# Keys turned with the heads innermost, moved in one piece, and read by the scores with a stride of 16 numbers

## The chip, the cores and the metric

The kernel runs on one core of a Trainium2 chip. The metric is the time of one execution on the device in microseconds (us), as the median of several runs; lower is better. One execution was recorded by the hardware profiler, and the views below come from it.

## The reference

There are two blocks, one after the other. The first is a gated linear attention over 4 batches, 8 heads, 768 steps and 48 numbers a head: a complex gate of magnitude at most 0.999 multiplies a 48 x 48 state at each step, and the query reads the state. The second is a layer of 3072 tokens, 384 numbers and 2048 hidden units, gated by the cosine.

```python
mag = np.sqrt(a_re * a_re + a_im * a_im)
scale = np.minimum(mag, 0.999) / (mag + 1e-06)
a_re_n, a_im_n = (a_re * scale, a_im * scale)
for t in range(S):
    ar, ai = (a_re_n[:, :, t, :, None], a_im_n[:, :, t, :, None])
    new_re = ar * S_re - ai * S_im
    new_im = ar * S_im + ai * S_re
    kv = np.einsum('bhd,bhe->bhde', k[:, :, t], v[:, :, t])
    S_re, S_im = (new_re + kv, new_im)
    y[:, :, t] = np.einsum('bhd,bhde->bhe', q[:, :, t], S_re)
...
h = x @ w_in            # x: y with the heads side by side
g = h * np.cos(h)
return (g @ w_out)
```

## The kernel before

The steps are cut into 24 chunks of 128, and two chunks make a group, so there are 12 groups (`G` = 2, `NG` = 12). Within a chunk the recurrence becomes matrix products. The gates are summed up as logarithms and angles, the keys are divided and the queries multiplied by the products of the gates, and each is stacked with its cosine and sine part into 96 numbers a head: `ks` and `qs`, 128 steps by 16 heads (8 heads of two chunks) by 96. The scores of a head (`sc`, `f_scores`) are the product of its turned keys and turned queries over the 96 numbers; VectorE masks them (`atm`), and they multiply `v` (`yp`, `f_out`). What came before the chunk is carried in `state` (`sp`, `state_sums` and `state_next`). The result goes through DRAM into `xT`, and then through the layer: `hp` (`mm1_sums`), the gate (sine and square on ScalarE, `gate_product` on VectorE), and the second product as `op` and `sum`, which from group 2 on is formed from seven products of half size.

`hp` of a group is made in eight pairs of 12 matmul records each; from group 2 on the three PSUM buffers of the pool `pm` are taken in turn, so the fourth pair needs the buffer of the first. Each fp32 matmul appears as two records, and so does each weight load.

The scores need the keys and queries turned, with the 96 numbers over the partitions and the 128 steps in a row. For groups 0 and 1 (`g < PEG`) TensorE turns them (`f_turn`), and ScalarE copies them out of PSUM. For groups 2 to 11 `f_transpose` does it in three steps, keys first, then queries:

- VectorE turns blocks of 32 x 32 into `tr`: 128 partitions (four quarters `q` of 32 steps, `r` within the quarter being one of the 96 numbers by threes), `NB` = 3 blocks, 16 heads `x`, 32 steps `j`.
- A DMA from the SP queue writes `tr` to DRAM, as `moved`, ordered by quarter and by number.
- DMAs from the SP queue read it back into `kT` or `qT`, 96 partitions.

`kT` is stored as heads, quarters, steps, so that the 128 columns of a head lie side by side; this takes four DMAs, one for each quarter. `qT` is stored as quarters, heads, steps and takes one; a head's 128 steps are then four runs of 32. In the scores `kT` is the stationary operand, and `qT` the moving one:

```python
matmul(ps[:, h], lhsT=X[n // G]["kT"][:, n % G * H + head],
       rhs=queries(n, head), start=True, stop=True)
```

`kT`, `qT` and `tr` have one, one and two buffers, `moved` three. TensorE's order is written out by `chain` in `matmul`. From group 2 on the program is woven: `weave` gives each part of a group's round a place between 0 and 1 and sorts by it. The scores of group n (`chunks(n)`) lie at the start, the layer's `hp` (`first(n)`) at 0.56 to 1, and the turning for group n + 1 (`keys(n + 1)`) at about 0.53 to 0.64, beside the first pairs of `hp`. VectorE and ScalarE take what the scheduler gives them in that order. SP's queue holds all loads, the transfers of the turning, those of `xT` and the stores.

Of the kernel before, what the change touches and what calls it, by code (L numbers as in the profile page):

```python
# [11 lines left out]
F32 = mybir.dt.float32  # L12
# [475 lines left out]
def fast_path(ctx, tc, q, k, v, a_re, a_im, moe_w_in, moe_w_out, out, least, odd, wide,  # L488
# [7 lines left out]
    nc = tc.nc  # L496
    B, H, S, D = q.shape
    DM, DF = moe_w_in.shape
    C = 128
    NCH = S // C  # L500
    G = 2
    N = B * NCH
    NG = N // G
    D2 = 2 * D
    HH = H // 2
    ND = DM // C
    Q4 = C // 32
    NB = D2 // 32
# [7 lines left out]
    ft = ctx.enter_context(tc.tile_pool(name="ft", bufs=2))  # L516
    msb = ctx.enter_context(tc.tile_pool(name="msb", bufs=2))
    rows_d = ctx.enter_context(tc.tile_pool(name="rows_d", bufs=2, space=bass.MemoryType.DRAM))
# [18 lines left out]
    def chain(ins, engine="scalar"):  # L537

        if engine in tail:
            behind(ins, tail[engine])  # L540
        tail[engine] = ins

    def behind(ins, other):
        tc.add_manual_dep(ins.ins, other.ins.name, mybir.DependencyInfo(
            mybir.DependencyClass.NoSync, mybir.DependencyReason.DATA))
# [14 lines left out]
    X = [dict() for _ in range(NG)]  # L560
# [4 lines left out]
    PEG, PER = 2, 1  # L565
# [118 lines left out]
    vector, scalar = Ordered(nc.vector, "vector"), Ordered(nc.scalar, "scalar")  # L684

    def matmul(out, **kw):
        chain(nc.tensor.matmul(out, **kw), "tensor")  # L687
# [233 lines left out]
    def f_transpose(g, i, n, name):  # L921


        if i == 0:
            X[g][name] = ft.tile([D2, G * H, Q4, 32] if name == "kT" else [D2, Q4, G * H, 32], F32,
                                 tag=name, name=name, bufs=1)
        tr = ft.tile([C, NB, n * H, 32], F32, tag="tr", name="tr")
        turn = vector.transpose(out=tr, in_=X[g][name[0] + "s"][:, ds(i * H, n * H)].rearrange(
            "p x a d -> p x (a d)").rearrange("p x (r b) -> p b x r", b=NB))
        if name == "qT" and "gated" in X[g - 1]:  # L930
            behind(turn, X[g - 1]["gated"])
        moved = rows_d.tile([Q4, D2, n * H, 32], F32, tag="moved", name="moved", bufs=3)
        nc.sync.dma_start(out=moved.rearrange("q (r b) x j -> (q r) b x j", b=NB), in_=tr)
        if name == "kT":
            for q4 in range(Q4):
                nc.sync.dma_start(out=X[g][name][:, ds(i * H, n * H), q4], in_=moved[q4])
        else:
            nc.sync.dma_start(out=X[g][name][:, :, ds(i * H, n * H)],
                              in_=moved.rearrange("q c x j -> c q x j"))

    def f_turn(g, i, name, hh):

# [9 lines left out]
    def queries(n, h):  # L952
        g, i = divmod(n, G)
        if g < PEG:
            return X[g]["qT"][:, i * H + h].rearrange("p q j -> p (q j)")
        return X[g]["qT"][:, :, i * H + h]

    def f_scores(n, hh):
        y = Y[n]
        if hh == 0:  # L960
            y["atm"] = ft.tile([C, H, C], F32, tag="atm", name="atm")
        ps = pa.tile([C, HH, C], F32, tag="a", name="sc")
        for h in range(HH):
            head = hh * HH + h
            matmul(ps[:, h], lhsT=X[n // G]["kT"][:, n % G * H + head],
                   rhs=queries(n, head), start=True, stop=True)
        y["masked"] = vector.tensor_tensor(
            out=y["atm"][:, ts(hh, HH)], in0=ps, in1=causal.unsqueeze(1).to_broadcast([C, HH, C]), op=ALU.mult)

    def f_out(n):  # L970
        y, (g, i) = Y[n], divmod(n, G)
        vals = X[g]["v"][:, i]
        state = y.get("state")
        if i == 0:
            X[g]["yT"] = ft.tile([C, HH, G, C], F32, tag="yT", name="yT", bufs=1)
        ps = pa.tile([C, HH, C], F32, tag="a", name="yp")
        for p in range(HH):
            for side in range(2):
                matmul(ps[ds(side * 64, D), p], lhsT=vals[:, 2 * p + side],
                       rhs=y["atm"][:, 2 * p + side], start=True, stop=(state is None))  # L980
            if state is not None:
                for side in range(2):
                    matmul(ps[ds(side * 64, D), p], lhsT=state[:, 2 * p + side],
                           rhs=queries(n, 2 * p + side), start=False, stop=True)
        for side in range(2):
            half = ds(side * 64, D)
            scalar.copy(out=X[g]["yT"][half, :, i], in_=ps[half])

    def f_rows(n, lo=0, hi=H):

        y, (g, i) = Y[n], divmod(n, G)
        state = y.get("state")
        if lo == 0:
            y["yr"] = pa.tile([C, H, D], F32, tag="a", name="yr")
        ps = y["yr"]
        for h in range(lo, hi):
            matmul(ps[:, h], lhsT=y["atm"][:, h], rhs=X[g]["v"][:, i, h],
                   start=True, stop=(state is None))
            if state is not None:
                matmul(ps[:, h], lhsT=queries(n, h), rhs=state[:, h], start=False, stop=True)  # L1000
        if hi < H:
            return
        y["rows"] = msb.tile([C, DM], F32, tag="ot", name="rows")
        scalar.copy(out=y["rows"], in_=ps.rearrange("p h d -> p (h d)"))
# [221 lines left out]
    def keys(g):  # L1226

        if not 0 <= g < NG:
            return
        for i, n in spans(g):  # L1230
            yield lambda i=i, n=n: g_trig(g, i, n)
            yield lambda i=i, n=n: (g_stack(g, i, n), p_end(g, i, n))
            for name in "kT", "qT":
                if g >= PEG:
                    yield lambda i=i, n=n, name=name: f_transpose(g, i, n, name)
# [24 lines left out]
    def chunks(g):  # L1260
        for n in range(g * G, g * G + G):
            for hh in range(2):
                yield lambda n=n, hh=hh: f_scores(n, hh)
            yield lambda n=n: f_state(n)
            yield lambda n=n: f_out(n)
        yield lambda: (f_x(g), f_xt(g))
        if g + 2 < NG:
            yield lambda: load(g + 2, ("k", "q", "v"))
# [101 lines left out]
    lows(0, 1)  # L1370
    piece(0)
    f_scores(0, 0)
    f_scores(0, 1)
    turn(0, 1)
    piece(0, 1, 0, 1)
# [302 lines left out]
```

## Time and profile before

| what | us |
|---|---|
| median of 3 runs | 655.88 |
| lowest and highest | 655.13, 659.32 |
| the profiled execution | 653.01 |
| its span in the trace | 651.2 |
| TensorE busy | 641.0 |
| VectorE busy | 492.0 |
| ScalarE busy | 392.8 |
| one turning of keys on VectorE, x10 | 2.252 |
| one issue of a kT DMA on SP, median, x40 | 1.323 |
| one issue of a qT DMA on SP, median, x10 | 1.185 |

Busy time is the sum of an engine's records; records of TensorE overlap, and the ends of its matmuls are modelled, so its pace is better read from the starts of successive records. In the profile, PE is TensorE's matmul, PEld its weight load, DVE is VectorE, ACT ScalarE, and SPq the DMA issue on SyncE's queue. Most operations go through two helpers and so carry line L687 (matmuls) or L676 (VectorE and ScalarE); tile names tell them apart. A group of records shows its count, then busy time and the mean length of one in ns, then the idle time ahead of it and what ended that idle time.

### The profile page before, as it was taken

To read this page: it belongs to the slowest core of one execution; us is meant where nothing else is said; L and a number is where in the kernel's file an instruction comes from. 1 tells how busy PE (TensorE), PEld (TensorE's weight loads), DVE (VectorE), ACT (ScalarE), POOL (GpSimd) and SP (SyncE) were. 2 spreads that over 40 slices of the span, in tenths; PEclk is the share of its full clock that TensorE was granted. 3 is DMA by queue.
4 is the path that set the end of the run, shared out by engine and by line. 5 is a ranking of instruction groups with operands and counts; after the bars stand their busy time and mean duration, and the time that the engine had idled before them with its cause. 6 is when DMAs were issued, how large, how long until landed. Compare 5 with 4: busy or idle time off the path is not lost.

```text
span 651.2 us, 10758 instructions
## 1 busy us (share of the span) xinstructions
PE 641.0 (98%) x4075; PEld 576.4 (89%) x4075; DVE 492.0 (76%) x799; ACT 392.8 (60%) x726; POOL 30.9 (5%) x53
## 2 busy tenths in 40 slices
PE   8999999999999999999999999999999999999997
PEld 6888877777999999899899899899899999999996
DVE  6999989888687688786787787876877878862251
ACT  7898687284583593494494485485576476433330
POOL 4010200000000000010010010000000000000000
PEclk9999999999999999999999999999999999999999
DMA  9968755727627656747738737836836843363001
GB/s 249 244 179 203 225 164 123 170 62 182 146 49 182 158 146 148 194 110 167 209 82 191 204 85 167 205 96 151 226 105 146 219 123 98 112 134 120 25 1 31
DMA packets 232920, 94.90 MB, mean 146 GB/s; under 512 B 208701, under 2 KB 221246, under 8 KB 232858
## 3 DMA queue, kind: packets, MB, share of 16 engines
q1 hardware_dynamic: 225320, 68.51, 45.3%
q0 software_dynamic: 5824, 25.50, 11.7%
q8 instruction: 34, 0.56, 0.4%
q10 hardware_dynamic: 1714, 0.11, 0.2%
q14 instruction: 28, 0.23, 0.1%
HBM read 69.28 MB, written 24.81 MB: 144 GB/s over the span
## 4 chain that ended last, share of the span: by engine, by line
PE 92%; ACT 4%; DVE 3%; DMA 0%; issue 0%; SPq 0%; DVEq 0%
PE hp L687 38%; PE op L687 18%; PE sum L687 16%; PE sc L687 6%; PE yp L687 6%; PE sp L687 4%; PE phs L687 2%; PE lgs L687 1%; ACT tan L707 1%; PE yr L687 1%; PE tp L948 1%; ACT rs L707 1%; ACT lg L707 1%; ACT L703 1%; DVE mag L676 1%; DVE atm L676 1%
## 5 line engine op out<-in xcount | busy, mean ns | idle before, releaser
L687 PE MATMUL hp<-xT,w_in 128*128 128x256 f32 (+1 forms) x1176 | 252.5, 375 | 0.0
L687 PEld LDWEIGHTS hp<-xT,w_in 128*128 128x128 f32 x1176 | 219.6, 190 | 30.2 <-issue 0.2
L707 ACT ACTIVATE gate<-hp,half_pi_b 128x512 f32<-128x512 f32 x96 | 66.0, 687 | 118.5 <-PE hp L687 118.5
L687 PE MATMUL op<-w_out,gate 128*128 128x192 f32 (+1 forms) x448 | 100.7, 374 | 0.0
L676 DVE TENSOR_TENSOR gate<-hp,gate 128x512 f32<-128x512 f32 x96 | 65.7, 684 | 45.8 <-ACT junk L676 45.7
L687 PEld LDWEIGHTS op<-w_out,gate 128*128 128x128 f32 x448 | 75.9, 190 | 16.9 <-issue 2.0
L676 ACT ACTIVATE junk<-hp 128x512 bf16<-128x512 f32 x96 | 56.7, 591 | 0.0
L687 PE MATMUL sum<-t_s,s 128*128 128x192 f32 x320 | 56.3, 329 | 0.0
L687 PEld LDWEIGHTS sum<-t_s,s 128*128 128x128 f32 x320 | 52.1, 190 | 1.5 <-issue 1.5
L676 DVE TENSOR_TENSOR atm<-sc,causal 128x512 f32<-128x512 f32 x48 | 32.9, 689 | 23.4 <-PE sc L687 23.4
L687 PEld LDWEIGHTS sc<-qT,kT 96*128 96x128 f32 x384 | 47.4, 192 | 2.3 <-issue 0.6
L687 PE MATMUL sc<-qT,kT 96*128 96x128 f32 x384 | 49.0, 276 | 0.2 <-ACT qT L676 0.2
L676 ACT ACTIVATE ot<-sum 128x192 f32<-128x192 f32 x39 | 12.6, 322 | 53.7 <-PE sum L687 53.4
L676 DVE SCALAR_TENSOR_TENSOR ot<-op,ot 128x192 f32<-128x192 f32 x40 | 13.3, 354 | 38.0 <-PE op L687 36.4
L687 PE MATMUL yp<-atm,v 128*48 128x128 f32 x352 | 33.6, 277 | 0.9 <-ACT Q L707 0.6
L703 ACT ACT_TABLE_LOAD x24 | 30.8, 1283 | 1.2 <-PEq L1662 0.7
L676 ACT COPY yT<-yp 48x512 f32<-48x512 f32 x44 | 25.3, 574 | 7.4 <-PE yp L687 7.0
L687 PE MATMUL yp<-qT,state 96*48 96x128 f32 x304 | 29.7, 272 | 0.0
L687 PE MATMUL sum<-w_out,gate 128*128 128x192 f32 x160 | 29.7, 329 | 0.0
L687 PE MATMUL sp<-v,ks 128*96 128x48 f32 x320 | 29.7, 245 | 0.0
L687 PEld LDWEIGHTS sp<-v,ks 128*96 128x96 f32 x320 | 29.6, 165 | 0.0
L676 ACT CAST tan<-phs 128x384 int32<-128x384 f32 x24 | 11.4, 480 | 29.4 <-PE phs L687 29.4
(147 smaller groups left out, 987.4 us busy)
## 6 DMA issues: line engine op xcount, KB each, us to landing
moved<-tr SPq DMA_DIRECT2D x20, 768.0 KB
raw<-in_moe_w_in_dram POOLq DMA_DIRECT2D x16, 768.0 KB, 5.1
raw<-in_moe_w_out_dram POOLq DMA_DIRECT2D x16, 768.0 KB, 4.6
kT<-moved SPq DMA_DIRECT2D x40, 192.0 KB
qT<-moved SPq DMA_DIRECT2D x10, 768.0 KB
k<-in_k_dram SPq DMA_DIRECT2D x24, 192.0 KB
q<-in_q_dram SPq DMA_DIRECT2D x24, 192.0 KB
v<-in_v_dram SPq DMA_DIRECT2D x24, 192.0 KB
```

The lines of the kernel that those rows point to most:

```text
L676: ins = getattr(self.engine, op)(**kw)
L687: chain(nc.tensor.matmul(out, **kw), "tensor")
L703: chain(nc.scalar.preload_act_table_set(table))
L707: chain(nc.scalar.activation(func=func, **kw))
L948: chain(nc.tensor.transpose(ps[:, h], X[g][name[0] + "s"][:, x0 + h].rearrange("p a d -> p (a d)"), ident), "tensor")
```

## The change

VectorE writes the turned keys with the 16 heads innermost: `tr`, `moved` and `kT` hold, for each step, the 16 heads side by side. The queries keep the order that they had. `moved` and the two turned tiles are now declared flat, and keys, like queries, are read back by one DMA whose pieces are the 512 numbers of a quarter. A head's keys are then every sixteenth number of a partition, over all 128 steps, and `turned_keys` gives the scores that view as the stationary operand. Groups 0 and 1 keep their layout.

```diff
         if i == 0:
-            X[g][name] = ft.tile([D2, G * H, Q4, 32] if name == "kT" else [D2, Q4, G * H, 32], F32,
-                                 tag=name, name=name, bufs=1)
-        tr = ft.tile([C, NB, n * H, 32], F32, tag="tr", name="tr")
-        turn = vector.transpose(out=tr, in_=X[g][name[0] + "s"][:, ds(i * H, n * H)].rearrange(
+            X[g][name] = ft.tile([D2, Q4, 32 * G * H], F32, tag=name, name=name, bufs=1)
+        tr = ft.tile([C, NB, 32 * n * H], F32, tag="tr", name="tr")
+        order = "p b (j x) -> p b x j" if name == "kT" else "p b (x j) -> p b x j"
+        turn = vector.transpose(out=tr.rearrange(order, j=32), in_=X[g][name[0] + "s"][:, ds(i * H, n * H)].rearrange(
             "p x a d -> p x (a d)").rearrange("p x (r b) -> p b x r", b=NB))
         if name == "qT" and "gated" in X[g - 1]:
             behind(turn, X[g - 1]["gated"])
-        moved = rows_d.tile([Q4, D2, n * H, 32], F32, tag="moved", name="moved", bufs=3)
-        nc.sync.dma_start(out=moved.rearrange("q (r b) x j -> (q r) b x j", b=NB), in_=tr)
-        if name == "kT":
-            for q4 in range(Q4):
-                nc.sync.dma_start(out=X[g][name][:, ds(i * H, n * H), q4], in_=moved[q4])
-        else:
-            nc.sync.dma_start(out=X[g][name][:, :, ds(i * H, n * H)],
-                              in_=moved.rearrange("q c x j -> c q x j"))
+        moved = rows_d.tile([Q4, D2, 32 * n * H], F32, tag="moved", name="moved", bufs=3)
+        nc.sync.dma_start(out=moved.rearrange("q (r b) y -> (q r) b y", b=NB), in_=tr)
+        nc.sync.dma_start(out=X[g][name], in_=moved.rearrange("q c y -> c q y"))
...
-        return X[g]["qT"][:, :, i * H + h]
+        return X[g]["qT"][:, :, ds((i * H + h) * 32, 32)]
+
+    def turned_keys(n, h):
+
+        g, i = divmod(n, G)
+        if g < PEG:
+            return X[g]["kT"][:, i * H + h].rearrange("p q j -> p (q j)")
+        return X[g]["kT"].rearrange("p q (j x) -> p (q j) x", j=32)[:, :, i * H + h]
...
-            matmul(ps[:, h], lhsT=X[n // G]["kT"][:, n % G * H + head],
+            matmul(ps[:, h], lhsT=turned_keys(n, head),
                    rhs=queries(n, head), start=True, stop=True)
```

## The prediction

> **What bounds the kernel now.** I read the totals by engine first, then the chain of waits, then TensorE's own waits, then TensorE in order of time around the scores, because only there does a record's real price show.
>
> ```profile
> PE 641.0 (98%) x4075; PEld 576.4 (89%) x4075; DVE 492.0 (76%) x799; ACT 392.8 (60%) x726; POOL 30.9 (5%) x53
> PE 92%; ACT 4%; DVE 3%; DMA 0%; issue 0%; SPq 0%; DVEq 0%
> ```
>
> The first line is busy time by engine, the second the chain that ended last. TensorE is busy for 641.0 of 651.2 us and is 92% of the chain; transfers are 0% of it. A busy TensorE may still be stalled, so the waits come next. These are all of its matmul side:
>
> ```profile
> PE busy L687 <- DVE one_b L557: 1.5, 1, 1.5
> PE phs L687 <- ACT tan L707: 1.4, 2, 0.8
> PE yp L687 <- ACT Q L707: 0.6, 1, 0.6
> PE tp L948 <- DVE ks L676: 0.6, 2, 0.4
> PE phs L687 <- DVE tan L676: 0.5, 1, 0.5
> PE yp L687 <- DVE atm L676: 0.3, 1, 0.3
> PE sc L687 <- ACT qT L676: 0.2, 1, 0.2
> ```
>
> No DMA is among them. The last line belongs to the first two groups, whose keys ScalarE copies, so the transfers of kT cost TensorE nothing today. What is left to read is its pace, from the timeline of TensorE in one steady group (start, length, records):
>
> ```profile
> 182.85 1.95 PE L687 MATMUL sc<-qT,kT 96*128 96x128 f32 x16
> 184.63 1.47 PE L687 MATMUL op<-w_out,gate 128*128 128x192 f32 x8
> 185.94 1.48 PE L687 MATMUL sp<-v,ks 128*96 128x48 f32 x16
> 187.24 0.42 PE L687 MATMUL lgs<-hi,exact 128*128 128x384 f32 x1
> 204.16 20.88 PE L687 MATMUL hp<-xT,w_in 128*128 128x256 f32 x96
> 224.88 1.06 PE L687 MATMUL sc<-qT,kT 96*128 96x128 f32 x8
> ```
>
> From start to start: hp takes 20.72/96 = 216 ns a record, so a moving column costs 0.84 ns. The sp records move only 48 columns (40 ns) yet take 1.30/16 = 81 ns: they are paced by their weight load, 96 columns at 0.84 ns, and that load runs beside the matmul before it. The scores take 1.78/16 = 111 ns: 128 moving columns want 108 ns and 128 weight columns want 108 ns as well. **The weight load of the scores is therefore exactly covered, with no slack.** Each head is two records[...], so 4 heads are 8 records.
>
> [...] The new stationary operand steps 16 numbers, 64 bytes[...]. The trace of before has no TensorE operand with such a step. It has one VectorE operand[...], the turning itself, which reads with a step of 3 numbers:
>
> ```profile
> L676 DVE STREAM_TRANSPOSE tr<-ks 128x1536 f32<-128x1536 f32 x10 | 22.5, 2252 | 0.0
> L676 DVE TENSOR_TENSOR mag<-mag,tan 128x768 f32<-128x768 f32 x11 | 10.5, 952 | 1.8 <-ACT tan L707 1.6
> L676 DVE TENSOR_TENSOR s<-gate,s 128x256 f32<-128x256 f32 x40 | 16.7, 418 | 0.0
> L687 PEld LDWEIGHTS sc<-qT,kT 96*128 96x128 f32 x384 | 47.4, 192 | 2.3 <-issue 0.6 <-ACT qT L676 0.5
> ```
>
> The two tensor operations give 534/512 = 1.04 ns an element and 152 ns fixed, so 1536 elements should take 1750 ns; the turning takes 2252, some 500 ns more. [...] That the 500 ns are the turning's own cost[...] remains possible.
>
> **The change part by part.**
>
> *Scores.* Ten groups (2 to 11) use the new layout; groups 0 and 1 are turned by TensorE and keep theirs. That is 32 of the 384 score records a group, 320 in all. With 1.69 ns a column a load takes 216 ns against a matmul of 108, so the pace goes from 111 to about 219 ns: 108 more each. A burst's first load runs beside the instruction before it. In a group the bursts are 8 after hp (216 ns, all covered), 8 after sum and 16 after op (both 192 columns, 163 ns: 54 uncovered). So 7 + 7 + 15 = 29 records at 108, plus 2 x 54: 3.24 us a group, 32.4 in ten; group 2 runs its bursts behind 384 columns and saves 0.1. What follows a burst loads at most 128 dense columns beside a score's 108 ns, at no cost. **+32 us, all on TensorE's path.** The lower bound is 0 (TensorE reads a number at a time and doesn't care), the upper a line at twice my estimate, since a step of 64 bytes is far beyond the 12 that the trace shows: 432 ns a load, 29 x 321 + 216 + 2 x 269 = 10.1 us a group, +101 us. A gain is excluded: 128 moving columns stay.
>
> *VectorE.* The keys' turning now writes with a step of 64 bytes. At 1.69 ns an element beside its reads it takes 1536 x 1.69 + 152 = 2.75 us, 0.5 more; bounds 2.25 (writes are free) and 3.85 (one more cycle for each write). I take 2.75. Behind it in VectorE's order stand the first gate product of hp, then the turning of qs, then the second product. In one steady group, by the timeline:
>
> ```profile
> 255.37 20.88 PE L687 MATMUL hp<-xT,w_in 128*128 128x256 f32 x96
> 258.50 2.24 DVE L676 STREAM_TRANSPOSE tr<-ks 128x1536 f32<-128x1536 f32 x1
> 260.73 0.67 DVE L676 TENSOR_TENSOR gate<-hp,gate 128x512 f32<-128x512 f32 x1
> 264.01 4.99 SPq L936 DMA_DIRECT2D kT<-moved  x4
> 269.11 1.38 SPq L938 DMA_DIRECT2D qT<-moved  x1
> 276.09 1.06 PE L687 MATMUL sc<-qT,kT 96*128 96x128 f32 x8
> ```
>
> The first product must release its PSUM buffer for the fourth pair of hp, which starts 36 records in, at 255.37 + 7.77 = 263.14; it ends at 261.40. The second ends at 264.14 for the fifth, at 265.73. So 1.6 us are covered, and 0.5 costs nothing; each 0.1 us beyond 1.6 would cost 0.1 us a group.
>
> *Transfers.* Ten groups issue four DMAs for kT, 96 x 16 pieces of 128 bytes each, 61,440 of the SP queue's 225,320 packets; after, one of 96 x 4 pieces of 2 KB. SP spends 4.99 us on the four and will spend about what qT takes, 1.4, so kT and qT are both issued some 3.6 us earlier, less the 0.5 of the turning. The round through DRAM stays. Today qT is issued by 270.49 and the scores start at 276.09 without waiting. Earlier arrival is worth nothing; fewer packets neither, for hp keeps 216 ns a record whatever the queues do.
>
> *Sum.* On the profiled execution's own 653.0 us: + 32 - 0 + 0 = 685. The median of the runs, 655.9, lies 2.9 above it, so 688. ScalarE and VectorE gain slack in the score stage, and masking waits longer for the scores; TensorE has op, sum or sp between scores and yp.
>
> **The rivals.** *The step is free* (0.20): TensorE fetches one fp32 number per 0.84 ns whatever its address[...]. For it: [...]all TensorE streams in this trace run at one and the same rate[...]. The scores stay at 111 ns, the transfers and VectorE are covered, and the time is 656. This is the case of the other side. Its place is the weight column: the scores are slower only if a column costs more than 111/128 = 0.87 ns, and I would see 1% (6.6 us) from 6.6/300 = 22 ns a record, 1.04 ns a column.
>
> *Lines dearer than estimated* (0.10): conflicts at 64 bytes, or writes of the turning that exceed the cover by over 1 us a group as well; 700 to 757, 725 in its middle. For it, only that no row shows such a step.
>
> *Half the penalty* (0.04): [...]a column costs 1.26 ns, or 161 ns; 29 x 52 = 1.5 us a group, 671.
>
> The transfers as a gain get 0.02: TensorE's waits hold 5.1 us in all, none on kT, so over 1% can hardly come.
>
> **How the numbers follow.** The doubled load has 0.64, predicted 688; its own range is 677 to 695, from columns of 1.4 ns (a pace of 182, 2.1 us a group) to 1.85 ns (240, 3.9 us). To leave out no more than 2 in 10, the range must take in the free case, which has 656, and the half penalty: 654 to 697, with 2 us at each end for the spread of the runs. The dearer case stays outside above. Slower by over 1% is 0.64 + 0.10 + 0.04 = 0.78; within 1% 0.20; faster by over 1% 0.02. About 1% is what a measurement of this kernel can tell from no change.
>
> **What would show it.** In the changed trace, 16 scores should span 3.4 us instead of 1.78, 8 after hp about 1.75, with hp at 216 and sp at 81 ns as before. The turning of ks should read 2.7 us, that of qs 2.25. SP should show one kT issue near 1.4 us. TensorE's waits should still name no transfer. If the scores keep 111 ns, the estimate of a line is wrong for TensorE and the forecast with it; if hp bursts lengthen past 20.9 us, VectorE's cover was too thin.

## The result, and the profile after

The changed kernel takes 684.1 us, median of four runs (683.11 to 684.48), against 655.5 us for the kernel before (654.37 to 659.32). The ratio is 1.0423, with a 95% interval of 1.0379 to 1.0467: slower, by 28.6 us between the medians. The profiled executions are 684.48 and 653.01 us, 31.5 us apart, and their spans, 682.7 and 651.2 us, as well; TensorE's granted clock was 0.998 and 1.000 in them.

The page's totals by engine and chain of waits, as they were shown of before:

```profile
PE 672.1 (98%) x4075; PEld 609.6 (89%) x4075; DVE 496.9 (73%) x799; ACT 393.6 (58%) x726; POOL 31.5 (5%) x53
PE 96%; ACT 2%; DVE 1%; DMA 1%; issue 0%; DVEq 0%
```

TensorE's busy time has grown by 31.1 us, as much as the span by 31.5. The number of records is the same. VectorE has 4.9 us more, ScalarE 0.8. TensorE's own waits are no longer than they were, 4.6 us in all in place of 5.1:

```profile
PE busy L687 <- DVE one_b L557: 1.5, 1, 1.5
PE phs L687 <- ACT tan L707: 1.4, 2, 0.8
PE tp L943 <- DVE ks L676: 0.6, 2, 0.4
PE phs L687 <- DVE tan L676: 0.5, 1, 0.5
PE hp L687 <- DMA xT<-x: 0.3, 1, 0.3
PE sc L687 <- ACT qT L676: 0.3, 1, 0.3
```

So the loss is no wait; TensorE is slower at something. Which thing is seen in its timeline, in the group that was shown of before, here from its first scores on:

```profile
177.25 1.80 PE L687 MATMUL sc<-qT,kT 96*128 96x128 f32 x8
178.89 1.47 PE L687 MATMUL sum<-w_out,gate 128*128 128x192 f32 x8
180.19 1.86 PE L687 MATMUL sc<-qT,kT 96*128 96x128 f32 x8
181.89 1.48 PE L687 MATMUL sp<-v,ks 128*96 128x48 f32 x16
...
187.09 3.60 PE L687 MATMUL sc<-qT,kT 96*128 96x128 f32 x16
190.52 1.47 PE L687 MATMUL op<-w_out,gate 128*128 128x192 f32 x8
191.82 1.48 PE L687 MATMUL sp<-v,ks 128*96 128x48 f32 x16
193.13 0.42 PE L687 MATMUL lgs<-hi,exact 128*128 128x384 f32 x1
210.05 20.88 PE L687 MATMUL hp<-xT,w_in 128*128 128x256 f32 x96
230.77 1.80 PE L687 MATMUL sc<-qT,kT 96*128 96x128 f32 x8
```

From start to start, 16 scores take 3.43 us or 214 ns each, where they took 111. The rest keeps its pace: sp 1.31/16 = 82 ns, hp 20.72/96 = 216 ns. The three bursts of this group (8, 8 and 16 scores) took 0.90 + 0.89 + 1.78 = 3.57 us and take 1.64 + 1.70 + 3.43 = 6.77, so 3.20 us more. Summed from start to start over all bursts of groups 2 to 11, the scores take 67.6 us in place of 35.7, which is 31.9 more and the whole loss.

The 214 ns are the mean of a burst, and the burst's first interval is shorter (159 ns here): the first load starts at 186.93 and runs beside the op record ahead of the burst. A window that begins inside the burst has 13 records:

```profile
187.68 3.01 PE L687 MATMUL sc<-qT,kT 96*128 96x128 f32 x13
```

From there to the start of op at 190.52 it is 2.84/13 = 218 ns a record; in the kernel before the pace inside a burst is 112 ns. The record of the weight load shows the cost too, here in the answer for the tile kT (shortest, median and longest in ns; the median was 192):

```profile
L687 PEld LDWEIGHTS sc<-qT,kT x384: 185/311/316, 23.8 to 619.6; 96*128 96x128 f32 x192
```

VectorE and SP around one group's turning, from the timeline:

```profile
264.47 20.88 PE L687 MATMUL hp<-xT,w_in 128*128 128x256 f32 x96
267.61 2.83 DVE L676 STREAM_TRANSPOSE tr<-ks 128x1536 f32<-128x1536 f32 x1
270.32 0.67 DVE L676 TENSOR_TENSOR gate<-hp,gate 128x512 f32<-128x512 f32 x1
273.66 0.33 SPq L934 DMA_DIRECT2D kT<-moved  x1
277.31 0.32 SPq L934 DMA_DIRECT2D qT<-moved  x1
285.19 1.80 PE L687 MATMUL sc<-qT,kT 96*128 96x128 f32 x8
```

The turning of the keys takes 2.83 us in place of 2.24. The first gate product ends at 270.99, ahead of the fourth pair of hp, which is due at 264.47 + 7.77 = 272.24, and hp keeps its 20.72 us. The issue of kT takes 0.33 us and that of qT 0.32; in the group shown of before they took 4.99 (four) and 1.38.

### The profile page after: what moved, and what is told of

Its sections match the earlier page's. It is cut to its first block, busy times and chain, and to the rows that moved or that the text cites. A ratio compares the mean times of both kernels' runs of the same rounds, so it can differ in the third digit from the quotient of the medians.

```text
span 682.7 us, 10720 instructions
## 1 busy us (share of the span) xinstructions
PE 672.1 (98%) x4075; PEld 609.6 (89%) x4075; DVE 496.9 (73%) x799; ACT 393.6 (58%) x726; POOL 31.5 (5%) x53
## 4 chain that ended last, share of the span: by engine, by line
PE 96%; ACT 2%; DVE 1%; DMA 1%; issue 0%; DVEq 0%
PE hp L687 36%; PE op L687 18%; PE sum L687 15%; PE sc L687 11%; PE yp L687 6%; PE sp L687 4%; PE phs L687 2%; PE busy L687 1%; PE lgs L687 1%; PE yr L687 1%; PE tp L943 1%; DMA xT<-x 1%; ACT L703 0%; ACT tan L707 0%; DVE ks L676 0%; ACT lg L707 0%
## 5 line engine op out<-in xcount | busy, mean ns | idle before, releaser
L687 PEld LDWEIGHTS sc<-qT,kT 96*128 96x128 f32 x384 | 80.0, 290 | 1.6 <-ACT qT L676 0.5
L687 PE MATMUL sc<-qT,kT 96*128 96x128 f32 x384 | 80.9, 359 | 0.3 <-ACT qT L676 0.3
L676 DVE STREAM_TRANSPOSE tr<-ks 128x1536 f32<-128x1536 f32 x10 | 28.3, 2829 | 0.0
```

The source lines that it names most:

```text
L676: ins = getattr(self.engine, op)(**kw)
```

## Experiments

The theory is that the weight load of the scores pays for its step, and that the load alone does. The rivals are VectorE's stepped writes, and the new transfers. Where a kernel reads columns that belong to no single head, its masked scores are also scaled to almost nothing, by 2^-30 in place of 0.25; that line is left out of the code below.

**The step alone.**

```diff
-            matmul(ps[:, h], lhsT=X[n // G]["kT"][:, n % G * H + head],
+            keys_ = X[n // G]["kT"][:, n % G * H + head]
+            if n // G >= PEG:
+                keys_ = X[n // G]["kT"].rearrange("p x q j -> p (x q j)").rearrange(
+                    "p (y x) -> p y x", x=G * H)[:, :, n % G * H + head]
+            matmul(ps[:, h], lhsT=keys_,
                    rhs=queries(n, head), start=True, stop=True)
```

> The kernel before, but in groups 2 to 11 the scores read their 128 stationary columns with a step of 16 numbers from kT as it was stored before; everything ahead of the scores is unchanged. The columns then belong to no single head, so the masked scores are scaled to almost nothing (the part of the attention within a chunk is left out). Theory (the weight load with a step pays): scores at 214 ns a record as in the changed kernel, 3.2 us more a group, +32 us, about 1.045 times before. Rival (it is VectorE's stepped writes, or the transfers): scores at 111 ns, time as before.

Measured: 684.72 us against 654.27, ratio 1.0458 (1.0427 to 1.0489), and the scores at 3.44/16 = 215 ns, from the timeline:

```profile
186.66 3.60 PE L687 MATMUL sc<-qT,kT 96*128 96x128 f32 x16
190.10 1.47 PE L687 MATMUL op<-w_out,gate 128*128 128x192 f32 x8
```

The turning and the four transfers are those of before, and the whole loss is there. So the stepped writes and the transfers are not its cause.

**The layout alone.**

```diff
-        return X[g]["kT"].rearrange("p q (j x) -> p (q j) x", j=32)[:, :, i * H + h]
+        return X[g]["kT"].rearrange("p q y -> p (q y)")[:, ds((i * H + h) * C, C)]
```

> The changed kernel, with its stepped turning on VectorE and its single transfer of kT, but in groups 2 to 11 the scores read 128 columns that lie side by side. These columns belong to no single head, so the masked scores are scaled to almost nothing (the part of the attention within a chunk is left out). Theory: turning of the keys stays at 2.82 us and is covered, the transfer saves nothing: time as before within 1%, scores at 111 ns. Rival (the layout itself costs): part of the 28 us stays, above 662 us.

Measured: 653.78 us against 654.27, ratio 0.9988 (0.9979 to 0.9998). The timeline gives 1.79/16 = 112 ns for the scores:

```profile
183.07 1.95 PE L687 MATMUL sc<-qT,kT 96*128 96x128 f32 x16
184.86 1.47 PE L687 MATMUL op<-w_out,gate 128*128 128x192 f32 x8
```

and the answer for the tile tr shows that the dear turning is in it (shortest, median and longest in ns):

```profile
L676 DVE STREAM_TRANSPOSE tr<-ks x10: 2820/2830/2860, 108.8 to 562.5; 128x1536 f32<-128x1536 f32 x10
```

The other parts of the change, 10 x 0.58 = 5.8 us more of turning on VectorE included, cost nothing; they bring 0.1%, with 0.2% as the end of the interval. The two parts add up to the change within its interval.

**Ten steps of the stationary operand, and ten of the moving one.** In the first kernel `stepped` gives the scores their `lhsT`, in the second their `rhs`, each group with its own step:

```diff
+    STEPS = {2: 1, 3: 2, 4: 3, 5: 4, 6: 5, 7: 6, 8: 8, 9: 12, 10: 15, 11: 16}
+    def stepped(t, n, h):
+        flat_ = t.rearrange("p a b c -> p (a b c)")
+        step, at = STEPS[n // G], n % G * H + h
+        first_ = at * C if step == 1 else at
+        if step == 16:
+            return flat_.rearrange("p (y s) -> p y s", s=16)[:, :, at]
+        return flat_[:, first_:first_ + (C - 1) * step + 1:step]
...
+                keys_ = stepped(X[n // G]["kT"], n, head)
```

> The kernel before, with the step of the scores' stationary operand set group by group: groups 2 to 11 read with steps of 1, 2, 3, 4, 5, 6, 8, 12, 15 and 16 numbers (masked scores scaled to almost nothing, as the columns are no head's). Read from the pace of the 16 scores in a row of each group. Theory[...]: 111 ns for steps 1 and 2, about 160 for 3[...], 214 for 4 and all above. Rival 1[...]: 111 for 1 to 4, 214 from 5 on. Rival 2 (a conflict of certain distances): 4, 8, 12 and 16 differ from 5, 6 and 15.

> The kernel before, with the same ten steps, but on the moving operand of the scores: groups 2 to 11 read the 128 moving columns of qT with steps of 1, 2, 3, 4, 5, 6, 8, 12, 15 and 16 numbers, the stationary operand as before (masked scores scaled to almost nothing). Theory[...]: the same paces, 111, 111, 160, then 214. Rival (only the weight load fetches one number at a time): 111 for all steps.

Because steps of 4 and 8 came out dearer than 5 and 6, and 12 dearest, a further kernel tried the steps between:

> The kernel before, with the stationary step of the scores set to 7, 9, 10, 11, 12, 13, 14, 15, 4 and 8 numbers in groups 2 to 11 (masked scores scaled to almost nothing). Theory[...]: every group near 220 ns a record. Rival[...]: 12 again near 264 in another group than before, others between 214 and 264, with 4 and 8 near 230 in their new groups.

The timeline of the first kernel, bursts of 16 at steps 2, 3, 4 and 12, each with the record that follows it:

```profile
183.13 2.05 PE L687 MATMUL sc<-qT,kT 96*128 96x128 f32 x16
185.02 1.47 PE L687 MATMUL op<-w_out,gate 128*128 128x192 f32 x8
...
235.33 2.91 PE L687 MATMUL sc<-qT,kT 96*128 96x128 f32 x16
238.07 1.47 PE L687 MATMUL op<-w_out,gate 128*128 128x192 f32 x8
...
289.27 3.84 PE L687 MATMUL sc<-qT,kT 96*128 96x128 f32 x16
292.95 1.47 PE L687 MATMUL op<-w_out,gate 128*128 128x192 f32 x8
...
504.27 4.40 PE L687 MATMUL sc<-qT,kT 96*128 96x128 f32 x16
508.50 1.47 PE L687 MATMUL op<-w_out,gate 128*128 128x192 f32 x8
```

and of the second at step 4:

```profile
289.52 3.81 PE L687 MATMUL sc<-qT,kT 96*128 96x128 f32 x16
293.15 1.48 PE L687 MATMUL op<-w_out,gate 128*128 128x192 f32 x8
```

The means of these bursts are 118, 171, 230 and 264 ns a record, and 227 for the moving operand. They hold the shorter first interval, and in group 11 (step 16) a first interval that is 0.1 us longer in the kernel before as well. The table therefore has the pace inside the bursts: the median, in ns, from the start of one record to the next over all bursts of a group, without the first two intervals. Each kernel ran once, and only its pace is read; where a step was tried in two groups or two kernels (stationary 4, 8, 12, 15 and 16), they agree within 1 ns.

| step in numbers | 1 | 2 | 3 | 4 | 5 | 6 | 7 | 8 | 9 | 10 | 11 | 12 | 13 | 14 | 15 | 16 |
|---|---|---|---|---|---|---|---|---|---|---|---|---|---|---|---|---|
| stationary | 112 | 119 | 175 | 233 | 222 | 223 | 231 | 238 | 240 | 227 | 247 | 268 | 256 | 243 | 230 | 219 |
| moving | 112 | 114 | 172 | 227 | 230 | 227 | | 233 | | | | 226 | | | 220 | 218 |

At steps 1 to 4 the stair has the shape that was expected (111, 111, 160, 214), and for both operands, but it is 3 to 9% higher at 2, 3 and 4. From 2 to 4 each number more of step costs 56 and 58 ns for the stationary operand and 58 and 55 for the moving one; from 4 to 5 the pace no longer rises so (233 and 222, 227 and 230). So the row of columns is counted here in pieces of four numbers, the step at which that rise ends; where the prediction speaks of a line, it is read as such a piece. With steps of 2, 3 and 4 the 128 columns touch 64, 96 and 128 pieces. Divided by these, the stationary operand takes 1.86, 1.82 and 1.82 ns a piece and the moving one 1.78, 1.79 and 1.77. So an estimate that fits the three steps is some 1.8 ns for each piece, whether one or two of its numbers are read; at step 1, with 32 pieces, the columns themselves set the pace (112/128 = 0.87 ns). With two numbers read of each piece the pace is thus nearly the dense one (119 and 114 ns against 112). The first rival, 111 ns for all steps up to 4, fails already at step 3, with 175 ns.

Beyond 4 the theory expected one price, and the step still matters: for the stationary operand the pace lies between 219 and 268 ns, and 12 costs 49 ns more than 16, with 11 and 13 between. For the moving operand it lies between 218 and 233, and 12 is not dear. Why is open.

**Steps on both operands.** The same helper, with a pair for each group.

> The kernel before, with steps on both operands of the scores, (stationary, moving) by group from 2 to 11: (1,1), (12,1), (2,16), (16,2), (8,8), (4,4), (16,16), (16,1), (3,3), (5,1) numbers, masked scores scaled to almost nothing. Theory (two streams side by side[...]): a pair costs what the dearer of the two costs alone: (2,16), (16,2), (8,8), (4,4), (16,16) about 220 to 235 ns a record, (3,3) about 170. Rival[...]: (8,8), (4,4) and (16,16) near 430. And for the 264 ns that a stationary step of 12 took in group 9: if the step makes it, (12,1) takes 264 here in group 3 and (16,1) in group 9 takes about 220; if the group's place does, the other way round.

Measured as in the table: (16,16) 217 ns, (2,16) 217, (16,2) 220, (4,4) 233, (8,8) 240, (3,3) 176, (5,1) 221, (1,1) 112; the timeline for (16,16):

```profile
458.04 3.66 PE L687 MATMUL sc<-qT,kT 96*128 96x128 f32 x16
461.53 1.48 PE L687 MATMUL op<-w_out,gate 128*128 128x192 f32 x8
```

Each pair takes what the dearer of its two takes alone, within 2 ns: both operands with a step of 16 take 217 ns and not twice as much. (12,1) took 268 ns in group 3 and (16,1) 218 in group 9, so the dear 12 is the step's and not the group's.

**What the turning pays.**

```diff
-        turn = vector.transpose(out=tr, in_=X[g][name[0] + "s"][:, ds(i * H, n * H)].rearrange(
-            "p x a d -> p x (a d)").rearrange("p x (r b) -> p b x r", b=NB))
+        src = X[g][name[0] + "s"][:, ds(i * H, n * H)].rearrange("p x a d -> p (x a d)").rearrange(
+            "p (b x r) -> p b x r", b=NB, r=32)
+        dst = tr
+        if name == "qT":
+            dst = tr.rearrange("p b x j -> p b (x j)").rearrange("p b (j x) -> p b x j", j=32)
+        turn = vector.transpose(out=dst, in_=src)
```

> The kernel before, but both turnings on VectorE read their 1536 numbers side by side (step 1 in place of 3); the turning of ks writes side by side, that of qs writes with a step of 16 numbers as the changed kernel's keys do (the keys and queries of groups 2 to 11 so become other numbers than a head's). Theory[...]: ks falls from 2.25 to 1.75 us, since 1536 x 1.04 + 152 ns is all that is left; qs stays near 2.82, set by its writes. Rival (the 500 ns are the turning's own): ks stays at 2.25.

The values it produces send the program on into its general path afterwards (2050.5 us in all), so its time says nothing; only the turnings are read, from the groups by form:

```profile
L676 DVE STREAM_TRANSPOSE tr<-qs 128x1536 f32<-128x1536 f32 x10 | 28.0, 2796 | 0.0
L676 DVE STREAM_TRANSPOSE tr<-ks 128x1536 f32<-128x1536 f32 x10 | 17.7, 1768 | 0.0
```

With dense reads and writes it takes 1.77 us (1.75 expected), so the 500 ns of before belong to reading with a step of 3 and not to the turning. Those reads touch 1536 x 3/4 = 1152 pieces of four numbers. With the prediction's estimate of 152 ns fixed, that is (2252 - 152)/1152 = 1.82 ns a piece, as much as TensorE's stationary operand takes at that step. With stepped writes and dense reads it takes 2.80, nearly as with stepped reads too (2.83): the two prices don't add up here either, and a write with a step of 16 costs, by the same estimate, (2796 - 152)/1536 = 1.72 ns (TensorE: 219/128 = 1.71).

**How much VectorE can take.**

```diff
+        if name == "kT":
+            turn = vector.transpose(out=tr, in_=X[g]["ks"][:, ds(i * H, n * H)].rearrange(
+                "p x a d -> p x (a d)").rearrange("p x (r b) -> p b x r", b=NB))
```

> The kernel before, with the turning of ks in groups 2 to 11 issued twice into the same tile: 2.2 us more on VectorE ahead of the first gate product of each group. Theory (1.6 us are covered by the PSUM buffers of hp): TensorE stalls at the fourth pair for about 0.6 us in each of nine or ten groups, +5 to +6 us, 1.008 to 1.009 times before. Rival 1 (the cover is larger): no change. Rival 2 (VectorE's time is on the path): +22 us, 1.034.

Measured: 670.31 against 654.54 us, ratio 1.0242 (1.0222 to 1.0261), +15.8 us. That lies between the theory and its second rival, and the theory's size is wrong. One group in the timeline:

```profile
259.14 7.93 PE L687 MATMUL hp<-xT,w_in 128*128 128x256 f32 x36
266.99 0.65 DVE L676 TENSOR_TENSOR gate<-hp,gate 128x512 f32<-128x512 f32 x1
267.69 13.37 PE L687 MATMUL hp<-xT,w_in 128*128 128x256 f32 x60 [0.62 <-DVE gate L676]
275.10 1.62 SPq L941 DMA_DIRECT2D qT<-moved  x1
281.73 1.13 PE L687 MATMUL sc<-qT,kT 96*128 96x128 f32 x8 [0.66 <-issue]
```

The fourth pair waits for the first product, as the theory says (due at 259.14 + 7.77 = 266.91, it starts at 267.69). But later pairs slip too, and the scores now wait. From the first hp record to the first score the nine groups take 15.4 us more than nine times 20.72. The idle times marked at the scores are 6.5 of it, in seven of nine groups, most of them put down to the transfer of qT; 8.9 are in hp, 1.0 a group. In these seven groups the scores start 4.7 to 5.6 us after the issue of qT has ended (here at 276.72, and the scores at 281.73).

**One transfer each way, with dense columns.** The DMA that writes `moved` puts the quarters side by side, and one DMA reads them back (the edit is to the changed kernel and is shown in part; the turning writes as it does for the queries, and the scores read 128 columns side by side):

```diff
+            moved = moved.rearrange("q c y -> (q c y)").rearrange("(c x q j) -> c x q j", c=D2, x=n * H, q=Q4)
+            nc.sync.dma_start(out=moved.rearrange("(r b) x q j -> q r (b x) j", b=NB),
+                              in_=tr.rearrange("p b (x j) -> p (b x) j", j=32))
+            nc.sync.dma_start(out=X[g][name].rearrange("c q y -> c (q y)"),
+                              in_=moved.rearrange("c x q j -> c (x q j)"))
```

> The keys keep the order of the queries on VectorE, the DMA that writes them to DRAM puts the four quarters of a head side by side (pieces of 128 bytes), and one DMA reads kT back in pieces of 8 KB: one transfer each way, and the scores read 128 columns side by side. Theory (transfers are off the path, steps are the whole loss): scores at 111 ns, time as before within 0.3%. Rival (the four transfers of before cost something after all): up to 0.3% faster than before, as the layout alone seemed to be by 0.1%. Rival 2 (128-byte writes to DRAM come late): slower than before.

Measured: 818.78 against 654.54 us, ratio 1.2523 (1.2479 to 1.2568): slower, as Rival 2 says. From TensorE's waits (us in total, times, longest):

```profile
PE sc L687 <- DMA qT<-moved: 138.5, 10, 14.4
```

and from the answer for the tile moved:

```profile
L934 SPq DMA_DIRECT2D moved<-tr x10: 567/601/632, 111.0 to 711.3; - x10
L939 SPq DMA_DIRECT2D moved<-tr x10: 15736/15922/16239, 113.7 to 714.0; - x10
```

The write of small pieces is issued in 0.6 us, but the next DMA on SP's queue, the write of the queries, then takes 15.9 us to issue, and every group's first scores wait some 14 us. The waits are 138.5 of the 164 us. The mean granted clock was 0.908, and the records behind such a wait are slow:

```profile
204.54 2.05 PE L687 MATMUL sc<-qT,kT 96*128 96x128 f32 x8 [13.78 <-DMA qT<-moved]
206.38 2.77 PE L687 MATMUL sum<-w_out,gate 128*128 128x192 f32 x8
208.94 1.57 PE L687 MATMUL sc<-qT,kT 96*128 96x128 f32 x8
...
211.67 1.53 PE L687 MATMUL sum<-w_out,gate 128*128 128x192 f32 x8
213.13 1.08 PE L687 MATMUL yp<-atm,v 128*48 128x128 f32 x16
```

From start to start, eight records of sum take 2.56 us right behind the wait and 1.46 after it, and the eight scores at 204.54 take 230 ns each. In the groups that begin at 204.54 and 271.28, the stretch from the first score to the op behind the 16 scores takes 12.80 and 12.77 us, in place of 10.07 and 10.96. If each of the ten groups loses some 2 us so, which is an estimate, it is most of the other 25. Whether the size of the pieces or their order over the four quarters makes the issue long was not tried.

**One issue in place of four.**

```diff
-            for q4 in range(Q4):
-                nc.sync.dma_start(out=X[g][name][:, ds(i * H, n * H), q4], in_=moved[q4])
+            nc.sync.dma_start(out=X[g][name][:, ds(i * H, n * H)],
+                              in_=moved.rearrange("q c x j -> c x q j"))
```

> The kernel before with one edit: the four DMAs that read kT back become one of four dimensions, still in pieces of 128 bytes and still with a head's 128 columns side by side. It takes from the change the single issue alone. Theory (neither the issues nor the pieces are on TensorE's path): scores at 111 ns a record, time as before within 0.3%. Rival 1 (four issues cost something): faster than before by 0.1 to 0.3%. Rival 2 (one large DMA of small pieces holds SP's queue, so that qT comes late): TensorE waits on the transfer of qT, slower by over 0.3%.

Measured: 656.08 against 654.83 us, ratio 1.0017 (1.0008 to 1.0026). The size is within the theory's 0.3%, but the wait that Rival 2 named is there. From TensorE's waits in the profiled execution, the slowest of 23 with 659.65 us:

```profile
PE sc L687 <- DMA qT<-moved: 1.6, 2, 0.8
```

and the tile moved:

```profile
L935 SPq DMA_DIRECT2D kT<-moved x10: 632/646/684, 116.3 to 574.0; - x10
L938 SPq DMA_DIRECT2D qT<-moved x10: 2199/2500/4171, 119.7 to 577.5; - x10
```

One issue of the same pieces takes 0.65 us, and that of qT, which is behind it and has not been changed, then 2.5 in place of 1.2 (medians). So the issue of qT took longer behind another DMA, though nothing of its own had changed; that both issues fell to 0.32 us in the changed kernel, where the pieces of kT are 2 KB, fits this.

No version here beats the kernel before by more than the 0.1% of the layout alone, and that one doesn't read the keys it should.

## Why the prediction was right, point by point

- **The scores.** Forecast a pace of 219 ns and 3.24 us a group; measured 219 inside the bursts and 3.2 in the group shown. The step alone carries the loss (684.72 us, 215 ns a score), so that the step is the cause is shown, not only fitted. The estimate of 1.69 ns a column came from VectorE and held for TensorE at this step: 219/128 = 1.71 ns.
- **What lies behind the estimate** had a doubt, that the turning's extra 500 ns were its own. They are not: with dense reads they are gone (1.77 us). But that the estimate came out so close is in part luck. The 1.69 ns are my estimate from the trace of before: 1.04 for a dense element, and 500/768 = 0.65 more, as if only half of the turning's 1536 elements paid for the step. That it is half of them was assumed and not shown; the stair says that each piece of four numbers costs about the same, and then the turning's own figure is 1.82 ns, which gives 233 ns for a load. That is what a step of 4 takes. A step of 16 happens to be the cheapest from 4 on; with 8, 9 or 11 to 14 (238 to 268 ns) a load takes more than the 1.85 ns a column where the prediction's own range for a doubled load ends.
- **The turning.** Forecast 2.75 us, measured 2.83, under the cover of 1.6 us; hp was not lengthened. How the cover ends was undersized: I priced only the fourth pair of hp, at 0.1 us for each 0.1 beyond 1.6, which gives 5 to 6 us for 2.2 us more. It cost 15.8. The missing terms are the later pairs (1.0 us a group in hp in all, in place of 0.6) and the wait of the scores for the transfer of qT (6.5 us).
- **The transfers.** Worth nothing, as forecast. But the reading behind it, qT issued 5.6 us ahead of the scores, made the slack look larger than it is: turning 2.2 us later makes the scores wait in seven of nine groups, 4.7 to 5.6 us after the issue of qT. The page doesn't give the landing for these DMAs; if it takes as long in the kernel before, an estimate, some 5 of those 5.6 us are the transfer, and only about half a microsecond was slack. In the changed kernel the issue of qT ended 2.0 us earlier after the start of hp and not 3.1 as the prediction's sum gives: SP's queue first waited for the queries to be written (in the group shown its issue of kT ends at 273.99, and that of qT starts at 277.31). The issue of kT was forecast near 1.4 us and is 0.32, since the 1.4 of qT, which I took for its price, was spent behind 128-byte pieces, as the kernel with one issue suggests.
- **Signs.** 16 scores were forecast at 3.4 us and take 3.43. For 8 after hp I wrote 1.75; my own sum gives 0.90 + 7 x 0.108 = 1.66, and 1.64 is measured. A wait on a transfer did appear, 0.3 us once on xT.
- **The sum.** On the profiled execution 685 was forecast and 684.5 measured. The median was forecast 2.9 us above that, since it lay so before; it is 0.4 below. That term, not the mechanism, makes up most of the distance from 688 to 684.1. The 2.9 came from three runs: over the 27 runs beside the last experiments the kernel before has a median of 654.83, 1.8 above the profiled execution.
- **The rivals.** A free step is excluded, and so is the half penalty at this step (161 ns), though step 3 (175 ns) comes near it. A dearer step exists, 12, but costs a quarter more (268 ns) and not twice.

## What to carry to other kernels

Here the weight load was as long as the matmul that covers it (both some 108 ns by the estimate, at a pace of 111), and a dearer read pattern was on the path at once (219 ns a record with a step of 16). So compare columns times the price of one with the pace from start to start before touching the layout, and read that pace inside a burst (218 ns here), behind its shorter first interval (159). In these runs fp32 operands could be read with a step of 2 for 2 to 7 ns a record (of 112), with 3 at about one and a half times the price, and from 4 on at 1.9 to 2.4 times the price. An estimate from VectorE's stepped read carried over to TensorE (1.69 ns a column against 1.71 at a step of 16), near enough to tell a doubling from no cost, but not to better than the spread from step to step (219 to 268 ns a record from 4 on). Fewer DMAs were worth 0.1% here (0.2% at the end of the interval), where TensorE waits on none of them; the pieces they are cut into went with how long the next issue in the queue took (0.32 us behind pieces of 2 KB, 1.2 to 2.5 behind pieces of 128 bytes), and slack in a queue is to be measured up to the landing and not to the issue (with the turning made twice, the scores that waited started 4.7 to 5.6 us after the issue of qT).

## What the runs showed of the hardware that was not expected

- From 2 to 4 numbers of step the pace goes with the count of pieces of four numbers that are touched, by the estimate above about 1.8 ns each, whether one or two numbers of it are read: 119, 175 and 233 ns a record for the stationary operand, 114, 172 and 227 for the moving one, 112 when dense.
- The price of a stationary step is not flat beyond 4 numbers: 222 ns a record at 5, 231 at 7, 268 at 12, 219 at 16, the same in two groups or more where it was repeated. For the moving operand 12 took 226. The cause is open.
- Stationary and moving operand, both with a step of 16, take 217 ns together, as one does alone.
- A DMA in 128-byte pieces, ordered over the four quarters first, made the DMA behind it in SP's queue take 15.9 us to issue, in place of the 0.33 us that the write of the queries takes to issue in the other kernels.
- In that kernel TensorE's mean granted clock was 0.908 in the profiled execution, and 0.998 to 1.000 in the runs of the kernel before. Behind a wait of 13.8 us, eight records of sum took 2.56 us there, and 1.46 later.
